# Seven block products for eight in the second layer's first multiplication, its sums by DMA

## The chip, the cores and the metric

One core of a Trainium2 chip runs the whole program. The metric is the time of one execution on the device, in microseconds; the figure for a kernel is the median of its runs. PE is TensorE, DVE is VectorE, ACT is ScalarE, POOL is GpSimd, SP the queue of SyncE.

## The reference

```python
# retention, then two gated layers; all float32 in the result
state = gamma * state + k[:, :, t] (x) v[:, :, t]          # per head, 768 steps
y[:, :, t] = scale * q[:, :, t] @ state
x  = y as (1536 tokens, 512)
x  = ((x @ w_a) * (x @ w_b)) @ w_out                      # 512 -> 1536 -> 512
h  = x @ w_in                                             # 512 -> 2048
g  = maximum(0.01 * h, h)
out = g @ w_out2                                          # 2048 -> 512
```

The weights arrive as 64-bit floats and are rounded to 32 bits on the chip.

## The kernel before

Activations lie transposed: a tile is 128 features by 512 tokens, so 1536 tokens are three token tiles (t = 0, 1, 2). Each float32 operand is split into a rounded high part and a remainder, and each product is three matmuls (`mm3`, lines 247 to 251: high x high, high x low, low x high). Every matmul of the two layers so has the line 249, 250 or 251; it moves 512 columns, or 256 where a half of token tile 1 is meant.

The stages follow each other on PE: retention until 47 us; x @ w_a and x @ w_b, twelve feature blocks, until 249 us; times w_out until 319 us; x @ w_in (here x is called y), sixteen feature blocks of 128, until 483 us; times the second w_out until the end.

Seven products for eight. The multiplications by the two w_out (class `Seven`, line 75) split tokens, the summed features and the outputs in halves, and replace eight half products by seven, p1, p7, p2, p6, p5, p4, p3, each over 6 (first layer) or 8 (second layer) steps j. One step is a product of 12 matmuls (6 of 512 columns, 6 of 256). For each, `items` (138) makes a form: three casts on ACT and three subtractions on DVE split the operands. After p1, p7 and p2 the operands themselves are summed in place (`sums`, 175, and `sum`, 117): in the first layer (`fold=True`) by DMAs that accumulate, issued by POOL (line 127), in the second by DVE (line 132). `combine` (795) adds the finished banks of p6 and p7 on DVE as soon as they are done (lines 802, 803).

The first layer's x @ w_a and x @ w_b already use seven block products for eight on the outer token tiles in feature blocks 3 to 10 (`fast`, 705): the columns of a and b are mixed and split (`sub_items`, 391), the mixed slices of x are made once (`mixed_items`, 682), and four of the products pass through one bank of PSUM, `top`, which ACT copies after the first three (723, 736, 742). Token tile 1 is done plainly. A step takes 66 matmuls of 512 columns, and one product of `Seven` is done between two steps. Tiles of the result that are not needed soon are stored to DRAM (`send`, 657) and come back later (`bring`, 665).

In the second layer x @ w_in is done plainly: `h2_step` (1054) does 12 matmuls for one token tile and one feature block, and ACT applies the rectifier (`Lrelu`, 1061) on the way out of the bank. After each feature block from the second on, one product of the second `Seven` is done, 15 in all; 41 follow.

Weights: `begin_steps` (289) has three ACT instructions (296, 299, 301: magnitude, sign, low word), `round_steps` (305) three of DVE (315 clamp, 317 shift and sign in one, 321 integer addition). Two blocks of the second layer are rounded in the first and parked in DRAM (`PARK`, line 43).

What sets the order: each engine runs its instructions in the order in which this program emits them. Work for ACT and DVE that belongs to later steps lies in the list `queue`, each item with a cost in us; `pump(us)` (333) emits items between groups of matmuls until their costs add up to its argument, and `until` (339) empties the queue as far as a needed item. `spare` is emitted when the queue is empty. On-chip tiles come from one pool of `NSLOT` buffers.

Of the kernel before, what the change touches and what calls it, by code (L numbers as in the profile page):

```python
# [14 lines left out]
U32 = mybir.dt.uint32  # L15
I64 = mybir.dt.int64
# [3 lines left out]
P = 128  # L20
# [3 lines left out]
TT = 512  # L24
# [7 lines left out]
NSLOT = 81  # L32
# [8 lines left out]
LEAD = 3  # L41
LEAD1 = 4
PARK = (0, 0, 0, 0, 0, 0, 0, 0, 0, 0, 0, 2)
# [4 lines left out]
AWAY = {(t, f) for t in range(3) for f in FAST if t == 2 or f >= FF1 // 2}  # L48
TOP = float(np.array((255 << 20) - 1, np.int32).view(np.float32))
# [25 lines left out]
class Seven:  # L75
# [17 lines left out]
    def __init__(self, nc, half, a, btile, form_new, banks, mm3, fold=False):  # L93
        self.nc, self.half, self.a, self.btile, self.fold = nc, half, a, btile, fold
# [9 lines left out]
    def away(self, i, k, j):  # L104

        return i and (2 * i, k * self.half + j) in AWAY and k == 0

# [9 lines left out]
    def sum(self, queue, op, j, d, x0, x1):  # L117
# [5 lines left out]
        if self.fold:  # L123
            for piece in range(2):
                if self.away(*d[1:], j) and not piece:
                    continue
                queue.append((0.0, lambda piece=piece: self.nc.gpsimd.dma_start(  # L127
                    self.A(*d[1:], j)[piece], self.A(*x1[1:], j)[piece], accum_op=ALU.add
                )))
            return  # L130
        for piece, cost in enumerate((0.61, 0.34)):
            queue.append((cost, lambda piece=piece: run(*(self.A(*x[1:], j)[piece] for x in (d, x0, x1)))))  # L132
# [42 lines left out]
    def sums(self, name, j):  # L175
        a11, a12, a21, a22 = (("A", i, k) for i in range(2) for k in range(2))
        b11, b12, b21, b22 = (("B", k, o) for k in range(2) for o in range(2))
        if self.fold and name in ("p1", "p7"):
            if name == "p1":
                self.sum(self.soon, "+", j, a11, a11, a21)  # L180
                self.sum(self.soon, "-", j, b11, b11, b12)
            else:
                self.sum(self.soon, "+", j, a11, a11, a22)
                self.sum(self.soon, "+", j, b12, b22, b11)
                self.sum(self.soon, "+", j, a21, a21, a22)
        elif name == "p1":
            self.sum(self.soon, "-", j, a11, a11, a21)
            self.sum(self.soon, "-", j, b11, b12, b11)
        elif name == "p7":
            self.sum(self.soon, "-", j, a11, a22, a11)  # L190
            self.sum(self.soon, "-", j, b12, b22, b11)
            self.sum(self.soon, "+", j, a21, a21, a22)
        elif name == "p2":
            self.sum(self.soon, "-", j, b21, b12, b21)
            self.sum(self.later, "-", j, a12, a12, a11)
            if j == self.half - 1:
                self.soon += self.later
# [24 lines left out]
def retention_moe_kernel(ctx: ExitStack, tc: tile.TileContext, ins, out):  # L222
# [33 lines left out]
    late_wi = [("wi", f) for f in range(FF2 - 4, FF2)]  # L256
    second = [(k, f) for f in range(FF2) for k in ("wi", "wq") if (k, f) not in late_wi]
    order, parked = [("a", 0), ("b", 0)], set()
    for f in range(1, FF1 + 1):
# [5 lines left out]
    order += second + late_wi  # L265
    source = {"a": (wab, 0), "b": (wab, 1), "wo": (wo, 0), "wi": (w2, 0), "wq": (w2, 1)}
    raws, begun, rounded, dram, signs = {}, {}, {}, {}, []
    at = {"load": 0, "begin": 0, "round": 0, "due": 0.0, "queued": 0}
# [10 lines left out]
    def word16(t, dtype, i):  # L279
# [9 lines left out]
    def begin_steps():  # L289
# [5 lines left out]
        low = tmp.tile([P, TT], I32, tag="low", name=f"low{n}")  # L295
        nc.scalar.activation(u, word(raw, F32, 1), AF.Abs, scale=2.0 ** -112)
        yield
        sign = signs[n % len(signs)]
# [3 lines left out]
        begun[key] = (u, low, sign)  # L302
        at["begin"] += 1

    def round_steps():
# [4 lines left out]
        if key not in begun:  # L310
            begin_weights()
        u, low, sign = begun.pop(key)
# [30 lines left out]
    def enqueue_round():  # L343
# [15 lines left out]
        items = [(0.05, begin), (0.46, step), (0.72, step), (0.95, end)]  # L359
# [5 lines left out]
    def enqueue_split(key, keep=False):  # L365
        def high():
            weights[key] = slots.new(F32R, f"{key[0]}{key[1]}h"), slots.new(F32R, f"{key[0]}{key[1]}l")
            nc.scalar.copy(weights[key][0], rounded[key])

        def low():  # L370
            src = rounded.pop(key)
            if key[0] == "a" and keep:
# [9 lines left out]
        behind.extend([(0.05, high), (0.05 if key[0] == "a" and keep else 0.61, low)])  # L382

    def enqueue_next(f):
        for k in "ab":
            enqueue_round()
            enqueue_split((k, f), f in FAST)
# [3 lines left out]
    def sub_items(f):  # L391

        def run(d, x, y):
            nc.vector.tensor_sub(*(kept[k, f][:, i * QT:(i + 1) * QT] for k, i in (d, x, y)))

        for d, x, y in (
            (("a", 0), ("b", 0), ("a", 0)),
            (("b", 0), ("b", 1), ("b", 0)),
            (("b", 1), ("b", 1), ("a", 0)),
            (("a", 1), ("a", 1), ("b", 1)),  # L400
# [3 lines left out]
        for k in "ba":  # L404
            def high(k=k):
                weights["t" + k, f] = slots.new(F32R, f"t{k}{f}h"), slots.new(F32R, f"t{k}{f}l")
                nc.scalar.copy(weights["t" + k, f][0], kept[k, f])

            def low(k=k):
                nc.vector.tensor_sub(weights["t" + k, f][1], kept.pop((k, f)), as32(weights["t" + k, f][0]))  # L410
# [3 lines left out]
            yield 0.61, low  # L414

# [27 lines left out]

    def ahead(rate, reserve, end):
        at["due"] = min(at["due"] + rate, 3.0)
        while at["due"] >= 1 and at["round"] < min(at["load"], end) and slots.room() >= 1 + reserve:
            round_weights()
            at["due"] -= 1
            if at["begin"] < min(at["load"], end):
                begin_weights()  # L450
# [204 lines left out]
    far, back = {}, []  # L655

    def send(t, f):

        if (t, f) in AWAY:
            far[t, f] = park.tile([P, TT], F32, tag=f"h{t}{f}", name=f"far{t}{f}")  # L660
            nc.gpsimd.dma_start(far[t, f], h[t, f])  # L661
            h[t, f] = far[t, f]
            slots.done(1)

    def bring(reserve=0):

        for key in list(far)[:1]:
            if slots.room() <= reserve:
                return
            h[key] = slots.new(F32, f"h{key[0]}{key[1]}")  # L670
            nc.sync.dma_start(h[key], far.pop(key))
            if key[0] == 2 and key[1] < FF1 // 2:
                back.append(key)

    def add_back():
        for _, f in back:
            nc.gpsimd.dma_start(h[2, f], h[2, f + FF1 // 2], accum_op=ALU.add)
        back.clear()

    S = {}  # L680

    def mixed_items():
# [9 lines left out]
        for j in range(2):  # L692
            for n, key in ((1, (2, 2 + j)), (3, (2, j)), (2, (0, j)), (4, (0, 2 + j))):
                def high(n=n, key=key, j=j):
                    S[n, j] = slots.new(F32R, f"s{n}{j}h"), slots.new(F32R, f"s{n}{j}l")
# [9 lines left out]
    def fast(f):  # L705

        def product(ps, key, half, xs, first, more):
            w = weights[key, f]
# [4 lines left out]
        copy, mul, add = nc.scalar.copy, nc.vector.tensor_mul, nc.vector.tensor_add  # L713
        a, b = range(2), range(2, KC)
        for t in range(NTILE):
            h[t, f] = slots.new(F32, f"h{t}{f}")
        want("a", f)
        pa = bank(f"pa{f}")
        ab_mm(pa, 1, f, 0, a)
        yield  # L720
        top, left = bank(f"top{f}"), bank(f"left{f}")
        product(top, "a", 0, [x[0, 0], x[0, 1]], True, False)
        copy(h[0, f], top)
        product(left, "a", 1, [x[0, 2], x[0, 3]], True, False)
        pump(2.0)
        add(h[0, f], h[0, f], left)
        ab_mm(pa, 1, f, 0, b)
        signed(h[1, f], pa, 1)
# [4 lines left out]
        until(lambda: ("ta", f) in weights and ("a", f) not in kept)  # L733
        product(top, "tb", 1, [S[2, 0], S[2, 1]], False, True)
        u = slots.new(F32, f"u{f}")
        copy(u, top)
        mid, pb = bank(f"mid{f}"), bank(f"pb{f}")
        product(mid, "ta", 0, [S[1, 0], S[1, 1]], True, False)
        ab_mm(pb, 1, f, 1, a)
        pump(3.3)  # L740
        product(top, "tb", 0, [S[3, 0], S[3, 1]], False, True)
        copy(h[2, f], top)
        slots.done(4)
        slots.tick()
        ab_mm(pb, 1, f, 1, b)
        pump(0.6)
        add(h[2, f], h[2, f], mid)
        pump(0.7)
        mul(h[1, f], h[1, f], pb)
        send(1, f)  # L750
# [3 lines left out]
        product(top, "ta", 1, [x[2, 2], x[2, 3]], False, True)  # L754
        pump(1.3)
        nc.vector.scalar_tensor_tensor(h[2, f], h[2, f], -1.0, top, op0=ALU.mult, op1=ALU.mult)  # L756
        send(2, f)
        product(mid, "b", 1, [S[4, 0], S[4, 1]], False, True)
        pump(1.0)
        add(u, u, mid)  # L760
        mul(h[0, f], h[0, f], u)
        send(0, f)
        slots.done(5)
        slots.tick()

# [447 lines left out]
```

## Time and profile before

| | us |
|---|---|
| median of 3 runs | 575.17 |
| lowest, highest | 574.05, 575.22 |
| profiled execution | 574.53 |
| its span | 572.8 |
| PE busy in the span | 567.5 |
| DVE busy | 447.8 |
| ACT busy | 371.9 |
| POOL busy | 82.7 |

The span runs from the first to the last instruction that the profile holds; the execution's time has some 1.7 us around it. Busy time is summed by engine; PE's end of a matmul is modelled, so the start times of successive matmuls say more than their durations. POOL's busy time is nearly all issuing of DMAs here.

### The profile page before, as it was taken

How to read it: one execution, taken by the hardware profiler on the slowest of the kernel's cores; microseconds unless marked ns; L12 is line 12 of the kernel's file. 1: busy time of each engine (PE TensorE's matmuls, PEld its weight loads, DVE VectorE, ACT ScalarE, POOL GpSimd, SP SyncE). 2: the span in 40 equal slices, each digit the busy share in tenths (PEclk: the TensorE clock that was granted, in tenths of full speed). 3: DMA queues.
4: the chain of work that ended last, by engine and by line, in shares of the span. 5: the costliest groups of instructions: out<-in, count | busy, mean ns of one | idle time of the engine just before them, and what ended most of it. 6: DMA issues, size and time to landing. Idle time of an engine off the chain costs nothing.

```text
span 572.8 us, 9199 instructions
## 1 busy us (share of the span) xinstructions
PE 567.5 (99%) x3287; PEld 479.8 (84%) x3287; DVE 447.8 (78%) x901; ACT 371.9 (65%) x776; POOL 82.7 (14%) x104
## 2 busy tenths in 40 slices
PE   9999999999999999999999999999999999999997
PEld 5998888888888888888888888888888888888886
DVE  4986687897988876799699686776886567789992
ACT  4777466776776764787568587777673547698610
POOL 2431300103233211077700000000000000000000
PEclk9999999999999999999999999999999999999999
DMA  8994924557676554699960053434330000010111
GB/s 323 369 392 170 259 58 129 135 144 163 174 212 196 157 157 170 243 307 237 223 149 1 1 185 110 124 100 140 116 111 0 1 0 2 2 55 1 57 55 56
DMA packets 34189, 78.53 MB, mean 137 GB/s; under 512 B 3936, under 2 KB 8288, under 8 KB 34144
## 3 DMA queue, kind: packets, MB, share of 16 engines
q1 hardware_dynamic: 23040, 58.73, 30.3%
q0 software_dynamic: 10816, 18.88, 16.2%
q8 instruction: 26, 0.43, 0.3%
q10 hardware_dynamic: 288, 0.34, 0.2%
q14 instruction: 19, 0.16, 0.1%
HBM read 57.22 MB, written 8.39 MB: 115 GB/s over the span
## 4 chain that ended last, share of the span: by engine, by line
PE 99%; DVE 0%; issue 0%
PE blk L250 12%; PE blk L249 12%; PE blk L251 12%; PE h L250 8%; PE h L249 8%; PE h L251 8%; PE pa L249 3%; PE pa L250 3%; PE pb L250 3%; PE pa L251 3%; PE pb L251 3%; PE pb L249 3%; PE top L249 3%; PE top L250 3%; PE top L251 3%; PE sc L514 2%
## 5 line engine op out<-in xcount | busy, mean ns | idle before, releaser
L250 PE MATMUL blk<-form,form 128*128 128x512 f32 (+1 forms) x224 | 75.8, 338 | 0.0
L249 PE MATMUL blk<-form,form 128*128 128x512 f32 (+1 forms) x224 | 75.6, 337 | 0.0
L251 PE MATMUL blk<-form,form 128*128 128x512 f32 (+1 forms) x224 | 75.3, 336 | 0.0
L157 DVE TENSOR_TENSOR form<-g,form 128x512 fp32r<-128x512 f32 x112 | 57.3, 553 | 2.4 <-ACT form L151 0.7
L151 ACT CAST form<-g 128x512 fp32r<-128x512 f32 x112 | 52.6, 513 | 8.5 <-DVE g L132 6.4
L1061 ACT ACTIVATE g<-h 128x512 f32<-128x512 f32 x48 | 28.7, 598 | 44.2 <-PE h L251 44.2
L250 PE MATMUL blk<-forma,forma 128*128 128x512 f32 (+1 forms) x168 | 57.1, 340 | 0.1
L249 PE MATMUL blk<-forma,forma 128*128 128x512 f32 (+1 forms) x168 | 56.7, 338 | 0.0
L251 PE MATMUL blk<-forma,forma 128*128 128x512 f32 (+1 forms) x168 | 56.5, 336 | 0.0
L157 DVE TENSOR_TENSOR forma<-h,forma 128x512 fp32r<-128x512 f32 x84 | 42.9, 551 | 5.5 <-ACT forma L151 5.2
L249 PEld LDWEIGHTS blk<-form,form 128*128 128x128 f32 x224 | 42.5, 190 | 5.5
L250 PEld LDWEIGHTS blk<-form,form 128*128 128x128 f32 x224 | 42.5, 190 | 5.0
L251 PEld LDWEIGHTS blk<-form,form 128*128 128x128 f32 x224 | 42.3, 189 | 4.7
L157 DVE TENSOR_TENSOR form<-wq,form 128x256 fp32r<-128x256 f32 x56 | 23.6, 421 | 25.1 <-ACT form L151 24.5
L151 ACT CAST forma<-h 128x512 fp32r<-128x512 f32 x84 | 39.1, 512 | 5.4 <-DMA h<-h 5.2
L250 PEld LDWEIGHTS blk<-forma,forma 128*128 128x128 f32 x168 | 31.9, 190 | 4.2 <-DVE forma L157 0.7
L249 PEld LDWEIGHTS blk<-forma,forma 128*128 128x128 f32 x168 | 31.9, 190 | 4.0
L127 POOL DMA_DIRECT2D h<-h x34 | 34.0, 1102 | 8.1 <-DVE forma L157 4.1
L251 PEld LDWEIGHTS blk<-forma,forma 128*128 128x128 f32 x168 | 31.8, 189 | 3.4
L132 DVE TENSOR_TENSOR g<-g,g 128x512 f32<-128x512 f32 (+1 forms) x56 | 30.7, 571 | 0.5 <-ACT g L1061 0.5
L151 ACT CAST form<-wq 128x256 fp32r<-128x256 f32 x56 | 22.6, 404 | 5.0 <-PE blk L251 2.1
L661 POOL DMA_DIRECT2D far<-h x18 | 10.3, 574 | 98.5 <-DVE h L756 34.5
(3079 smaller groups left out, 1556.7 us busy)
## 6 DMA issues: line engine op xcount, KB each, us to landing
raw_wi<-in_w SPq DMA_DIRECT2D x16, 512.0 KB, 3.3
raw_wq<-in_w SPq DMA_DIRECT2D x16, 512.0 KB, 3.4
raw_a<-in_wab SPq DMA_DIRECT2D x12, 512.0 KB, 6.0
raw_b<-in_wab SPq DMA_DIRECT2D x12, 512.0 KB, 4.0
raw_wo<-in_wo SPq DMA_DIRECT2D x12, 512.0 KB, 5.1
far<-h POOLq DMA_DIRECT2D x18, 256.0 KB, 4.5
h<-far SPq DMA_DIRECT2D x18, 256.0 KB, 8.9
h<-far POOLq DMA_DIRECT2D x13, 256.0 KB, 8.9
```

The costliest lines, as they stand in the source:

```text
L127: queue.append((0.0, lambda piece=piece: self.nc.gpsimd.dma_start(self.A(*d[1:], j)[piece], self.A(*x1[1:], j)[piece], accum_op=ALU.add)))
L132: queue.append((cost, lambda piece=piece: run(*(self.A(*x[1:], j)[piece] for x in (d, x0, x1)))))
L151: nc.scalar.copy(h, src)
L157: nc.vector.tensor_sub(*todo.pop(0))
L249: nc.tensor.matmul(ps, w[0], x[0], start=first, stop=False, skip_group_check=more)
L250: nc.tensor.matmul(ps, w[0], x[1], start=False, stop=False, skip_group_check=more)
L251: nc.tensor.matmul(ps, w[1], x[0], start=False, stop=last, skip_group_check=more)
L514: nc.tensor.matmul(sc[h][:, c], d["k"][r, c], d["qs"][r, c], start=True, stop=True)
L661: nc.gpsimd.dma_start(far[t, f], h[t, f])
L1061: nc.scalar.activation(g[t, f], ps, AF.Lrelu, alpha=0.01)
```

## The change

Feature blocks 4 to 13 of x @ w_in are taken in five pairs (`PAIRS`), and each pair goes through the scheme that `fast` has for w_a and w_b; that scheme becomes `seven_for_eight`, with the work on each finished bank passed in. The other blocks, 0 to 3, 14 and 15, stay plain. The rectifier is `Prelu` with its slope as an operand; where a block is a sum of two banks, ACT copies the first, DVE adds the second, and ACT applies the rectifier in place. Half of the tiles of g get the opposite sign, so that all sums of g are additions, and these are done by accumulating DMAs from POOL as in the first layer, save one that stays on DVE (p2's, `here`). Tiles of g are stored to DRAM and brought back (`Away`). Eight products of the second `Seven` are done among the steps (numbers 0 to 7), 48 after them. The sums of p6's finished banks go into the queue in both layers. In rounding, sign and low word share one 32-bit tile, so that DVE shifts alone and adds once. In the first layer one more weight block is rounded and parked in each of the steps 5 to 10. The pool has 83 buffers for 81.

```diff
-NSLOT = 81
+NSLOT = 83
+PAIRS = range(2, 7)
+NWQ = (1, 3, 1, 1, 1, 1, 1, 4)
+SOON = 9
+FORM2 = ((), (), (0,), (1,), (2,), (3,), (4,), (5, 6))
+MAKE2 = ((), (), (0,), (1,), (2,), (3,), (4,), ())
+STEP2 = {(7, 1): 5, (7, 3): 6, (7, 5): 7}
+NMADE2 = 8
-PARK = (0, 0, 0, 0, 0, 0, 0, 0, 0, 0, 0, 2)
+PARK = (0, 0, 0, 0, 0, 1, 1, 1, 1, 1, 1, 2)
+AWAY2 = {(t, f) for t in range(3) for f in range(2 * PAIRS[-1] + 2) if t == 2 or f >= FF2 // 2}
...
         for piece, cost in enumerate((0.61, 0.34)):
-            queue.append((cost, lambda piece=piece: run(*(self.A(*x[1:], j)[piece] for x in (d, x0, x1)))))
+            if self.away(*d[1:], j) and not piece:
+                continue
+            if here:
+                queue.append((cost, lambda piece=piece: run(*(self.A(*x[1:], j)[piece] for x in (d, x0, x1)))))
+                continue
+            queue.append((0.0, lambda piece=piece: self.nc.gpsimd.dma_start(
+                self.A(*d[1:], j)[piece], self.A(*x1[1:], j)[piece], accum_op=ALU.add
+            )))
...
-        nc.scalar.mul(word16(sign, F16, 1), word(raw, F32, 1), 2.0 ** -100)
+        nc.scalar.mul(half(sl, F16, 1), word(raw, F32, 1), 2.0 ** -100)
         yield
-        nc.scalar.mul(low, word(raw, U32, 0), 2.0 ** -29)
+        nc.scalar.mul(half(sl, U16, 0), word(raw, U32, 0), 2.0 ** -29)
...
-        nc.vector.scalar_tensor_tensor(
-            ui, ui, 3, sign, op0=ALU.logical_shift_left, op1=ALU.bitwise_or
-        )
+        nc.vector.tensor_scalar(ui, ui, 3, None, op0=ALU.logical_shift_left)
         yield
-        nc.vector.tensor_tensor(ui, ui, low, op=ALU.add)
+        nc.vector.tensor_tensor(ui, ui, sl, op=ALU.add)
...
-        items = [(0.05, begin), (0.46, step), (0.72, step), (0.95, end)]
+        items = [(0.05, begin), (0.4, step), (0.4, step), (0.8, end)]
...
-            nc.scalar.copy(weights[key][0], rounded[key])
+            (nc.vector.tensor_copy if key[0] == "wi" else nc.scalar.copy)(weights[key][0], rounded[key])
...
+    def seven_for_eight(ka, kb, X, S, xf, ends):
+
+        s1, c11, ma, uu, u3, c22, mb, c21, c12 = ends
...
         product(top, ka, 0, [X[0, 0], X[0, 1]], True, False)
         s1(top)
         product(left, ka, 1, [X[0, 2], X[0, 3]], True, False)
         pump(2.0)
         c11(left)
         middle(pa, ka, b)
         ma(pa)
         pump(0.7)
...
         product(top, tb, 1, [S[2, 0], S[2, 1]], False, True)
         uu(top)
...
         if name == "p6":
             for m, ps in enumerate(z.acc[name]):
-                (sub if z.fold else add)(u["p1"][m], u["p1"][m], ps)
-                add(u["p7"][m], u["p7"][m], u["p1"][m])
+                p1, p7 = u["p1"][m], u["p7"][m]
+                queue.append((0.61, lambda p1=p1, ps=ps: sub(p1, p1, ps)))
+                queue.append((0.61, lambda p1=p1, p7=p7: add(p7, p7, p1)))
...
-        if n in (2 * H1 + 1, 4 * H1):
+        if n == 2 * H1 + 1:
             enqueue_round()
...
+    def leaky(d, src, t):
+
+        plus = {0: TT, 1: QT, 2: 0}[t]
+        if plus:
+            nc.scalar.activation(d[:, 0:plus], src[:, 0:plus], AF.Prelu, alpha=0.01)
+        if plus < TT:
+            nc.scalar.activation(d[:, plus:], src[:, plus:], AF.Prelu, scale=-0.01, alpha=100.0)
...
-        nc.scalar.activation(g[t, f], ps, AF.Lrelu, alpha=0.01)
...
+    def summed():
+        while sums2:
+            t, f = sums2.pop(0)
+            leaky(g[t, f], g[t, f], t)
+            gs.send(t, f)
+
+    def fast2(f):
+
+        def s1(top):
+            nc.scalar.copy(g_new(0, f), top)
+            summed()
+
+        def total(t, f, ps):
+            nc.vector.tensor_add(g[t, f], g[t, f], ps)
+            sums2.append((t, f))
+
+        def straight(t, f, ps):
+            leaky(g_new(t, f), ps, t)
+            gs.send(t, f)
+
+        def u3(top):
+            nc.scalar.copy(g_new(2, f + 1), top)
+            summed()
...
+        return seven_for_eight(("wi", f), ("wi", f + 1), y, SY, yf, (
...
+        if q in PAIRS:
+            now = fast2(f)
+            next(now)
+            if before:
+                next(before, None)
+                make2(MAKE2[q - 1])
+            next(now)
+            before = now
...
+            if q == HALF - 1:
+                fetch(1, 6)
+                for _ in range(2):
+                    gs.bring(6, False)
...
+    for n in range(NMADE2, len(z.plan) - 2):
+        for _ in range(2):
+            gs.bring(8, n >= 2 * HALF)
+        if n >= 2 * HALF:
+            gs.add_back(4 if n < 4 * HALF - 6 else 0)
...
+        pump(1.0)
```

## Rows read from the trace of the kernel before

**Rows 1.** Page, part 4: chain that ended last, by engine.

```profile
PE 99%; DVE 0%; issue 0%
```

**Rows 2.** Timeline of PE, x w_in: start us, us, engine, line, instruction.

```profile
339.11 0.40 PE L249 MATMUL h<-y000h,wi2h 128*128 128x512 f32 x1
...
347.30 0.39 PE L249 MATMUL blk<-form,form 128*128 128x512 f32 x1
...
349.37 0.40 PE L249 MATMUL h<-y000h,wi3h 128*128 128x512 f32 x1
```

**Rows 3.** Windows: length, busy (count) PE PEld DVE ACT POOL, clock, DMA share, GB/s.

```profile
112.55:231.98 119.43, 119.43 (x545) 99.39 (x544) 98.73 (x184) 79.25 (x151) 26.22 (x36) 1.00 0.63 173
...
249.14:318.67 69.53, 69.46 (x399) 60.68 (x398) 63.51 (x143) 47.05 (x114) 28.16 (x33) 1.00 0.74 157
318.67:483.15 164.48, 164.48 (x768) 137.83 (x767) 116.13 (x227) 108.68 (x210) 0.00 (x0) 1.00 0.24 77
483.15:569.45 86.30, 85.84 (x491) 75.19 (x490) 70.96 (x160) 49.05 (x119) 0.00 (x0) 1.00 0.09 33
```

**Rows 4.** Windows of two steps of seven products, first layer.

```profile
146.67:163.74 17.07, 17.07 (x80) 14.19 (x79) 15.78 (x30) 13.59 (x27) 4.87 (x7) 1.00 0.68 180
163.74:180.80 17.06, 17.06 (x80) 14.24 (x79) 13.96 (x28) 11.68 (x23) 4.39 (x6) 1.00 0.66 181
```

**Rows 5.** Timeline of PE at the first of two gaps.

```profile
290.75 0.39 PE L249 MATMUL blk<-forma,forma 128*128 128x512 f32 x1
291.17 0.50 PE L250 MATMUL blk<-forma,forma 128*128 128x512 f32 x1
```

**Rows 6.** Groups by line: busy us, mean ns | idle before, releaser.

```profile
L157 DVE TENSOR_TENSOR form<-g,form 128x512 fp32r<-128x512 f32 x112 | 57.3, 553 | 2.4 <-ACT form L151 0.7
...
L1061 ACT ACTIVATE g<-h 128x512 f32<-128x512 f32 x48 | 28.7, 598 | 44.2 <-PE h L251 44.2
L157 DVE TENSOR_TENSOR form<-wq,form 128x256 fp32r<-128x256 f32 x56 | 23.6, 421 | 25.1 <-ACT form L151 24.5
...
L299 ACT ACTIVATE sign<-raw_wi 128x512 f16<-128x512 f32 x16 | 12.5, 782 | 0.0
...
L317 DVE SCALAR_TENSOR_TENSOR wi<-wi,sign 128x512 int32<-128x512 int32 x16 | 11.1, 692 | 1.3 <-ACT sign L299 0.8
...
L321 DVE CUSTOM_DVE_ANT_0 wi<-wi,low 128x1024 uint16<-128x1024 uint16 x16 | 11.1, 691 | 0.8
...
L296 ACT ACTIVATE wi<-raw_wi 128x512 f32<-128x512 f32 x16 | 10.6, 660 | 0.0
...
L632 ACT ACTIVATE h<-pa 128x256 f32<-128x256 f32 (+1 forms) x16 | 7.0, 440 | 1.3 <-PE pa L251 1.3
...
L315 DVE TENSOR_SCALAR wi<-wi 128x512 f32<-128x512 f32 x16 | 6.7, 421 | 4.0 <-ACT wi L296 3.9
...
L726 DVE TENSOR_TENSOR h<-h,left 128x512 f32<-128x512 f32 x8 | 5.4, 679 | 0.0
...
L1061 ACT ACT_TABLE_LOAD x1 | 1.3, 1283 | 0.0
```

**Rows 7.** Timeline: copy of `top`, PE's next write there, two steps.

```profile
149.69 0.58 ACT L723 COPY h<-top 128x512 f32<-128x512 f32 x1
...
150.46 0.40 PE L249 MATMUL top<-s20h,tb6h 128*128 128x512 f32 x1
...
165.01 0.59 ACT L723 COPY h<-top 128x512 f32<-128x512 f32 x1 [0.17 <-PE top L251]
...
167.53 0.39 PE L249 MATMUL top<-s20h,tb7h 128*128 128x512 f32 x1
```

**Rows 8.** Source line 127, DMA sums: ns min/median/max, who waited, landing.

```profile
L127 POOL DMA_DIRECT2D h<-h x34: 853/1006/2634, 129.6 to 286.3; - x34
...
  ACT forma L151: 5.2, 4
...
DMA to landing us min/median/max: 4.5/8.3/11.6
```

More of the change, by code (lines that the diff above doesn't have):

```diff
@@ L711, in product, with middle @@
                 mm3(ps, (w[0][:, c], w[1][:, c]), xs[j], first and j == 0, j == 1, more)
-        copy, mul, add = nc.scalar.copy, nc.vector.tensor_mul, nc.vector.tensor_add
-        a, b = range(2), range(2, KC)
[L715 to L719, printed above, removed]
+        def middle(ps, key, kcs):
+            w = weights[key]
+            for kc in kcs:
+                c = slice(kc * P, (kc + 1) * P)
+                mm3(ps, (w[0][:, c], w[1][:, c]), X[1, kc], kc == 0, kc == KC - 1)
+        a, b = range(2), range(2, KC)
+        want(*ka)
+        pa = bank("pa")
+        middle(pa, ka, a)
         yield
[L721 to L724, printed above, removed]
+        top, left = bank("top"), bank("left")
+        product(top, ka, 0, [X[0, 0], X[0, 1]], True, False)
+        s1(top)
+        product(left, ka, 1, [X[0, 2], X[0, 3]], True, False)
         pump(2.0)
-        add(h[0, f], h[0, f], left)
-        ab_mm(pa, 1, f, 0, b)
-        signed(h[1, f], pa, 1)
+        c11(left)
+        middle(pa, ka, b)
+        ma(pa)
         pump(0.7)
@@ L732, in fast @@
             spare.pop(0)[1]()
[L733 to L739, printed above, removed]
+        until(lambda: ta in weights and ka not in kept)
+        product(top, tb, 1, [S[2, 0], S[2, 1]], False, True)
+        uu(top)
+        mid, pb = bank("mid"), bank("pb")
+        product(mid, ta, 0, [S[1, 0], S[1, 1]], True, False)
+        middle(pb, kb, a)
         pump(3.3)
-        product(top, "tb", 0, [S[3, 0], S[3, 1]], False, True)
-        copy(h[2, f], top)
+        product(top, tb, 0, [S[3, 0], S[3, 1]], False, True)
+        u3(top)
         slots.done(4)
         slots.tick()
-        ab_mm(pb, 1, f, 1, b)
+        middle(pb, kb, b)
         pump(0.6)
-        add(h[2, f], h[2, f], mid)
+        c22(mid)
         pump(0.7)
-        mul(h[1, f], h[1, f], pb)
-        send(1, f)
+        mb(pb)
         slots.tick()
@@ L993, in leave_part @@
             y_split(i, o, m, sums[m])
-            if op:
+            if m < 2:
+                if not op:
+                    yf[0, m] = slots.new(F32, f"yf{m}")
+                    nc.scalar.copy(yf[0, m], sums[m])
+                else:
+                    yf[2 * i, 2 * o + m] = sums[m]
+            elif op:
                 slots.done(1)
@@ L1132, in retention_moe_kernel, with make2 @@
-    for n in range(FF2 + 1, FF2 + LEAD - 1):
-        z.prep(n)
-    for n in range(FF2 - 1, len(z.plan) - 2):
+    def make2(ns):
+        for n in ns:
+            until(lambda: n in z.forms)
+            z.product(n)
+            pump(1.8)
+            queue.extend(z.soon)
+            z.soon.clear()
+    spare.extend(mixed_items(yf, SY, "r"))
+    before = None
+    for q in range(HALF):
+        f = 2 * q
+        for key in (("wi", f + 2), ("wi", f + 3)) if q + 1 < HALF else ():
+            if key in dram:
+                obtain(key)
+            if key not in rounded:
+                enqueue_round()
+            enqueue_split(key, q + 1 in PAIRS)
+        forms = list(FORM2[q])
+        if q == HALF - 1:
+            queue.extend(z.items(forms.pop(0)))
+        for n in range(max(NWQ[q], len(forms))):
+            if n < NWQ[q]:
+                enqueue_round()
+            if n < len(forms):
+                queue.append((0.0, lambda m=forms[n]: queue.__setitem__(slice(0, 0), z.items(m))))
+        queue.extend(behind)
+        behind.clear()
+        if q + 1 in PAIRS:
+            queue.extend(sub_items(("wi", f + 2), ("wi", f + 3)))
+        if q in PAIRS:
[6 more added lines that the diff above has]
+            before = now
+            if q == PAIRS[-1]:
+                make2(MAKE2[q])
+                next(now, None)
+                summed()
+                slots.done(16)
+                slots.tick()
+            continue
+        if q > PAIRS[-1]:
+            gs.arrange()
+        steps = [(t, f + i) for i in range(2) for t in range(NTILE)]
+        if not q:
+            steps = [(2, 0), (2, 1), (0, 0), (1, 0), (0, 1), (1, 1)]
+        for n, (t, ff) in enumerate(steps):
+            h2_step(t, ff, all(k[1] != ff for k in steps[n + 1:]))
+            slots.tick()
+            pump(2.5)
+            if q == HALF - 1:
+                fetch(1, 6)
+                for _ in range(2):
+                    gs.bring(6, False)
+            if (q, n) in STEP2:
+                make2([STEP2[q, n]])
+                if n == 1:
+                    queue.extend(z.items(NMADE2 - 1))
+                if n == 3:
+                    for m in range(LEAD):
+                        queue.extend(z.items(NMADE2 + m))
+                    queue.append((0.7, lambda: (z.early(LEAD), z.early(LEAD + 1))))
+        if q == HALF - 1:
+            keep(z, u2, "p1")
+        slots.tick()
```

300 lines of the change are left out of this document (148 added, 152 removed).

## The prediction

> **What bounds the kernel now.** The page's chain that ended last is PE for 99% [rows 1]. The page itself warns that a busy PE need not be a PE at its peak, so the second view was the order of time on PE [rows 2]. There the reader sees matmuls of 512 columns of x w_in: 36 of them from 339.11 to 347.30, so one each 0.2275 us, and then one product of the second large multiplication to 349.37, 2.07 us. Nothing lies between. The stages [rows 3] say the same: TensorE has the granted clock 1.00 (2.4 GHz) and is busy throughout, while in the stage of x w_in DVE is busy for 116.1 and ACT for 108.7 of 164.5 us. So a change gains here only if matmuls go, or one of the few gaps; and it loses where another engine delivers late.
>
> **What goes.** For each pair of feature blocks the outer token tiles (0 and 2) are now done with seven block products for eight. Of 2 blocks x 3 tiles x 4 slices x 3 matmuls = 72, the 24 of the middle tile stay and the other 48 become 7 x 2 x 3 = 42. Five pairs lose 5 x 6 = 30 matmuls of 512 columns. The same scheme already runs in the first layer, so its price on PE can be read: a step of it lasts 17.06 us [rows 4] and holds 66 such matmuls and one product, (17.06 - 2.07)/66 = 0.227 us each; the scheme adds nothing between them. 30 x 0.227 = 6.8 us.
>
> **A gap that goes.** In the first layer's multiplication PE waits twice for DVE, at 291.17 and in the same way at 293.58. The first of these starts 0.42 us after the one before [rows 5], not 0.2275, and the second 0.43: together 0.4 us. Ahead of the late operand DVE sums the finished banks of p6, six instructions at the 0.68 of an addition from PSUM [rows 6], 4.1 us in a row; the change puts these in the queue, one behind each product, and also rounds one weight block less in this stage. Then 0.4 us goes; 0 if the operand is late for ACT's sake.
>
> **What is added on PE.** Seven products that stood between the steps of x w_in move behind them. Between steps one costs 2.07 [rows 2], 41 in a row 86.30/41 = 2.10 [rows 3]: 7 x 0.03 = 0.2 us.
>
> **The other engines, second layer.** One step of a pair with its product is 66 x 0.227 + 2.07 = 17.06 us of PE. DVE, by [rows 6], a half width at 0.421, a full one in SBUF at 0.553, from PSUM at 0.679: three roundings of 0.421 + shift + 0.691; four half-width mixes, 1.7; four splits, each a copy and a subtraction; three sums from PSUM, 2.0; one form, 0.553 + 2 x 0.421; a half-width sum of w_out. The shift alone and the copy are not in the trace. The shift lies between 0.421 (one operand, as the clamp) and 0.692 (as now, with two), the copy between 0.421 and 0.553; I take 0.421 for both, since one operand in SBUF is the nearest. That makes 4.6 + 1.7 + 3.9 + 2.0 + 1.4 + 0.4 = 14.0 us, at the upper ends 15.4. ACT, a full width at 0.598 and a half at 0.440: three roundings of 0.660 + 0.782 + the third, between 0.660 and 0.782 (a 16-bit write as the second; taken), 6.7; a form 0.598 + 2 x 0.440 = 1.5; three copies of a bank, 1.8; the rectifier on four tiles and on four halves, 4.2. The slope operand's own cost is not in the trace; 0.44, a half, and 0.782, the dearest full width, bound it, and I take 0.598, the present rectifier. Together 14.2 of 17.06. Both fit. On the other side 48 sums of g leave DVE, 24 full at some 0.68 and 24 half at 0.42, 26 us in all. In their place POOL, which does nothing in these two stages [rows 3], issues 40 accumulating DMAs and 8 that add the parked tiles back.
>
> Two waits are new. The rectifier of a summed tile stands on ACT behind the next copy of a bank and waits for DVE's addition, with the next rounding queued behind it; the addition was emitted a group of products (1.4 us) earlier and takes 0.68, so I cost the wait at nothing, at most 0.7 where DVE is an instruction late, which falls into ACT's slack of 2.9 a step. And 26 tiles of g leave by POOL and come back on SP's queue, 12 of them before p2 reads them some 8 products (17 us) later; with the 8.3 us that DMAs take here [rows 8] they are in time, and behind them on SP stand only loads of w_out that were parked. The DMA engines are used for 0.24 and 0.09 of these stages.
>
> **First layer.** Six more blocks are rounded and parked, one in each step from block 5 to 10. Seven steps now have DVE busy for 98.7 and ACT for 79.3 of 119.4 us [rows 3], 14.1 and 11.3 a step. One rounding more, with the cheaper shift in all, gives DVE + 1.53 - 3 x 0.27 = 14.8 (15.9 if the shift stays at 0.692) and ACT + 2.2 + 3 x 0.12 = 13.9, also below 17.06. The parking is one issue on a POOL of which 26 of 119 us are used.
>
> **Where the cover is thin.** The average is not the test. The bank `top` takes four products in turn, and after the first ACT must have copied it before PE writes on: PE has two groups of six matmuls, 2.7 us, to do meanwhile. In the step where ACT was busy for 11.7 us the copy ended at 165.60 and PE came at 167.53: 1.9 us to spare. In the step where ACT was busy for 13.6 us it ended at 150.27 and PE came at 150.46: 0.19 us to spare [rows 4, 7]. By the sums above all eleven steps of both layers will have ACT at about 14. So I expect the copy close to its limit in all of them; with a scatter of a few tenths about a tenth of a microsecond each is lost, 1 us (an estimate from these rows). Its bounds are 0, and 2.0 a step, a whole rounding of 2.2 ahead of the copy less the 0.19: 22 us. I take the end that the rows are near.
>
> **POOL and the sums by DMA.** Sums of g now wait on POOL's queue, behind sends that wait for ACT's rectifier. The issue took 0.85 to 2.63 us, the middle value 1.0, and 8.3 us to land [rows 8]. p7 needs 24; the last that p6 reads is the 23rd, 23 x 1.0 + 8.3 = 31 us after the first, and that operand is wanted 23 products, 48 us, after it. In the first layer, with 18 sums and four products less between, ACT waited 5.2 us for such DMAs [rows 8] and PE lost 0.4 at most. I cost it at nothing; the cover is gone if an issue takes over (48 - 8.3)/23 = 1.7 us. The Trainium skill speaks against this part: in SBUF — State Buffer, section SBUF: two separate sides, it says that a DMA issued from GpSimd starves while DVE copies fp32 in SBUF in its two-port mode, and gives 620 ns alone and some 3100 ns beside such a copy. By its figure the 23 would take 71 us and be some 31 us late (an estimate from that page). The trace bears out a spread, not that mean: with DVE busy for 63.5 of 69.5 us [rows 3] the middle value stayed at 1.0.
>
> **Sum.** From the profiled execution, 574.53 us (span 572.8 and 1.7 around it): - 6.8 - 0.4 + 0.2 + 1.0 = - 6.0, 568.5 us. The median of the runs shown is 575.17, the lowest 574.05; the profiled one lies between, so I leave the number.
>
> **Rivals.** (1) Part of the gain is given back: the queue's order makes weights or copies late in some steps, 3 us more: 571.5. For it speaks the margin of 0.19 us [rows 7], against it seven steps at 17.06 with DVE at 83%. (2) Slower: ACT's copy of `top` is late in most steps because a rounding stands ahead of it. If half of the eleven steps have the margin 0.19 and half 1.9, a rounding of 2.2 costs 5.5 x 2.0 + 5.5 x 0.3 = 12.7 us: 567.5 + 12.7 = 580.2. It decides against the change from 7 us, 0.6 a step. For it rows 7, against it that ACT is idle for 3 us of 17. (3) Sums late: at the longest issue 23 x 2.63 + 8.3 = 69 us against 48, p6 waits 21 us, 589. (4) The new rectifier needs another table than copies and roundings. Now one load of 1.283 us stands before the first rectifier and none after [rows 6], with copies in between. If the two shared no table, some five groups a pair and 18 tiles outside would switch twice each, 86 x 1.283 = 110 us on an ACT with about 30 to spare: 80 us more, about 650. By the Trainium skill, ScalarE: Activation LUTs, section Table sets: the hidden batching unit, cheap functions stand in every set and only a change of set costs a load; the single load agrees for the present rectifier, and no row shows the new one. (5) More tiles are live at once, and a new one waits for the store of an old one, up to 8.3 us. One such wait would eat the gain: 574.5.
>
> **How the numbers follow.** Forecast 0.64, (1) 0.20, (2) 0.07, (3) 0.03, (4) 0.02, (5) 0.04. The forecast's own range is 567.0 (nothing late, and 0.5 less in all) to 570.0. For 8 in 10 the range must take in (1) to a microsecond above its value: 567.0 to 572.5. What this measurement can tell from no change is 0.2%, 1.2 us: faster means below 574.0. Forecast, (1) and half of (5) are faster, 0.86; the rest of (5) and 0.03 of (2), where it takes about 7, are the same, 0.05; the rest of (2), (3) and (4) are slower, 0.09.
>
> **What would show it.** PE should have 30 matmuls less; a pair of x w_in with a product should last 17.1 us; the two waits near 291 should be gone; POOL should be busy in the second layer; one table load. If the pairs last 18 us or more with PE waiting for `top`, rival 2 is true; if p6's forms wait for DMA, rival 3. The prediction is wrong if PE's gaps in the eleven steps add up to more than 4 us, or if no gap appears and the time is still above 570.

## The result, and the profile after

The changed kernel takes 566.81 us, median of four (566.14 to 567.27), beside 574.82 for the kernel before in the same runs: ratio 0.9861, 95% interval 0.9844 to 0.9878. That is 8.0 us less, where 6.0 to 6.7 were forecast (568.5 from 574.53 or 575.17), and 0.2 us below the range. The interval, put as a time, goes from 565.9 to 567.8, so this run does not tell the 0.2 from the range's end at 567.0. The page after, its span and part 1:

```profile
span 565.1 us, 9509 instructions
...
PE 559.8 (99%) x3257; PEld 473.7 (84%) x3257; DVE 449.1 (79%) x938; ACT 382.1 (68%) x802; POOL 144.9 (26%) x186
```

PE has the 30 matmuls less (3257 for 3287). The stages (length, busy time of PE, PEld, DVE, ACT, POOL, clock, DMA share, GB/s), as in [rows 3]:

```profile
112.80:232.20 119.40, 119.40 (x545) 99.36 (x544) 102.43 (x200) 91.48 (x169) 29.63 (x42) 1.00 0.74 213
...
249.40:318.30 68.90, 68.90 (x398) 60.62 (x398) 61.48 (x138) 46.63 (x113) 26.85 (x31) 1.00 0.82 179
318.30:461.30 143.00, 143.00 (x654) 119.26 (x653) 106.13 (x216) 95.63 (x190) 33.55 (x49) 1.00 0.60 177
461.30:562.30 101.00, 100.54 (x575) 88.06 (x574) 83.86 (x193) 59.33 (x147) 25.75 (x30) 1.00 0.56 126
```

The reader sees POOL come to work in both stages of the second layer, ACT go from 79.3 to 91.5 us in the seven steps of the first, and PE without idle time everywhere. Three steps of pairs of x w_in, windows as in [rows 4]:

```profile
371.80:388.86 17.06, 17.06 (x79) 14.23 (x79) 16.34 (x35) 13.64 (x27) 3.51 (x5) 1.00 0.65 173
388.86:405.92 17.06, 17.06 (x79) 14.23 (x79) 13.93 (x30) 11.79 (x24) 5.13 (x8) 1.00 0.73 209
...
422.98:440.04 17.06, 17.06 (x79) 14.21 (x79) 6.38 (x13) 7.84 (x17) 7.53 (x11) 1.00 0.92 303
```

They last 17.06 us, as the first layer's, though DVE is busy for 16.34 of them in the first of these. The two gaps of [rows 5] are gone. Where the cover was thought thin, at the copies of `top`, the instructions stand as follows, as in [rows 7]: one step of the first layer (block 6) and the second pair of the new stage.

```profile
148.21 0.59 ACT L801 COPY h<-top 128x512 f32<-128x512 f32 x1
...
150.73 0.39 PE L249 MATMUL top<-s20h,tb6h 128*128 128x512 f32 x1
...
374.67 0.57 ACT L1125 COPY g<-top 128x512 f32<-128x512 f32 x1
...
375.51 0.39 PE L249 MATMUL top<-r20h,twi7h 128*128 128x512 f32 x1
```

Block 6, where 0.19 us were to spare, now has 150.73 - 148.80 = 1.93; the new pair has 0.27. Single instructions against [rows 6] (mean ns):

```profile
L304 ACT ACTIVATE sl<-raw_wi 128x512 uint16<-128x512 uint32 x16 | 12.4, 772 | 0.0
...
L320 DVE TENSOR_SCALAR wi<-wi 128x512 int32<-128x512 int32 x16 | 6.8, 425 | 0.4
...
L1095 ACT ACTIVATE g<-top 128x512 f32<-128x512 f32 x5 | 2.9, 587 | 4.8 <-PE top L251 4.8
...
L866 ACT ACT_TABLE_LOAD x1 | 1.3, 1283 | 1.2 <-DVE warm L863 1.2
```

The shift alone takes 425 ns, the third rounding instruction 772, the rectifier 587 from a full bank: all near the values that were taken. The one table load stands at the start of the kernel (L866), where the kernel before has one as well; the one before the first rectifier is gone. The DMA sums of g (line 138), as in [rows 8]:

```profile
L138 POOL DMA_DIRECT2D g<-g x26: 860/1274/2871, 379.3 to 482.1; - x26
L138 POOL DMA_DIRECT2D g<-farg x14: 868/932/2787, 378.7 to 470.8; - x14
...
DMA to landing us min/median/max: 3.0/8.1/13.7
```

Where the 7.7 us between the two profiled spans lie, read from the starts of PE's instructions: from the first matmul of the first layer to the first of x w_in 273.92 before and 273.32 after (-0.60); from there to the last matmul of the kernel 247.99 and 241.19 (-6.80); from the end of the last addition to the end of the span (the tail) 3.31 and 2.76 (-0.55); the first matmul of the first layer starts at 46.80 and 47.05 (+0.25).

### The profile page after: what moved, and what is told of

Read it like the earlier page. It is cut to its first block, busy times and chain, and to the rows that moved or that the text cites. A ratio compares the mean times of both kernels' runs of the same rounds, so it can differ in the third digit from the quotient of the medians.

```text
span 565.1 us, 9509 instructions
## 1 busy us (share of the span) xinstructions
PE 559.8 (99%) x3257; PEld 473.7 (84%) x3257; DVE 449.1 (79%) x938; ACT 382.1 (68%) x802; POOL 144.9 (26%) x186
## 4 chain that ended last, share of the span: by engine, by line
PE 97%; DMA 2%; POOL 0%; SPq 0%; DVE 0%; issue 0%
PE blk L250 12%; PE blk L249 12%; PE blk L251 12%; PE top L249 4%; PE top L250 4%; PE top L251 4%; PE pa L249 4%; PE pa L250 4%; PE pb L250 4%; PE pa L251 4%; PE pb L249 4%; PE pb L251 4%; PE h L249 3%; PE h L251 3%; PE h L250 3%; PE mid L249 2%
## 5 line engine op out<-in xcount | busy, mean ns | idle before, releaser
L663 POOL DMA_DIRECT2D farg<-g x26 | 14.4, 557 | 114.0 <-ACT g L1095 97.6
L138 POOL DMA_DIRECT2D g<-g x26 | 29.5, 1651 | 3.2 <-DVE form L165 1.3
L663 POOL DMA_DIRECT2D farh<-h x18 | 10.3, 575 | 59.9 <-DVE h L791 36.1
```

What stands on the lines that cost most here:

```text
L663: nc.gpsimd.dma_start(self.far[t, f], self.tiles[t, f])
```

## The experiments

An experiment without a ratio is one profiled execution; it is read by stretches of its trace and not by its time.

**The changed kernel and the kernel before once more** (no edit).

> The changed kernel itself, once more. Theory: 30 matmuls (6.8 us) and two waits of PE (0.6) are all that the change gives, 7.4 us; the other 0.3 to 0.6 of the 8.0 between the medians is scatter at the beginning and the end of an execution. Then the ratio in five rounds is near 1 - 7.4/574.8 = 0.987, TensorE again enters x w_in 312 to 314 us before its last matmul with no gap of its own, and the start and the tail differ from the first profile by up to 0.5 us. Rival: some 0.6 us more are gained in a step that I have not seen; then the start and the tail repeat to 0.1 us and the ratio is 0.986 or less.

> The kernel before, once more, for the scatter of one profile against another: the first matmul of the first layer at 46.9 us and 3.35 us from the last addition to the end of the span in the first profile. Theory (scatter): both move by 0.2 to 0.5 us. Rival (the change moved them): both repeat to 0.1.

The changed kernel took 567.1 (ratio 0.987, 0.9852 to 0.9889), just inside the predicted range. Its profile has 273.28, 241.20 and 2.77 us for the three stretches; that of the kernel before has 274.16, 247.99 and 3.33. The first matmul of the first layer moved between 46.72 and 48.14: that is scatter. The first stretch of the kernel before moved too, by 0.24: its two waits are longer here, and the change gains 0.88 us in this stretch for 0.60 in the first pair of profiles. The tail did not move: 2.76 and 2.77 after, 3.31 and 3.33 before, so the scatter theory is wrong for it and the change has 0.55 us more there.

**Where the first layer's gap comes from.** One edit of the change each in the kernel before:

```diff
-                (sub if z.fold else add)(u["p1"][m], u["p1"][m], ps)
-                add(u["p7"][m], u["p7"][m], u["p1"][m])
+                p1, p7, op = u["p1"][m], u["p7"][m], sub if z.fold else add
+                queue.append((0.61, lambda p1=p1, ps=ps, op=op: op(p1, p1, ps)))
+                queue.append((0.61, lambda p1=p1, p7=p7: add(p7, p7, p1)))
...
+            until(lambda: name == "p2")
...
+        pump(1.0)
```

> The kernel before with one part of the change: the sums of p6's finished banks go through the queue, one or two behind each product, in both layers. Theory: PE's two waits at 291 and 294 us came from DVE doing six of these sums in a row ahead of the next form; they go, 0.6 us. Rival: the operand was late because ACT rounded a weight block at that place (and waited for a DMA before it); then the waits stay.

```diff
-        if n in (2 * H1 + 1, 4 * H1):
+        if n == 2 * H1 + 1:
```

> The kernel before with another part of the change: the second rounding of a weight block during the first layer's w_out (behind product 24) is left out there and done in the next stage. Theory (DVE's sums made the operand late): the two waits near 291 and 294 stay, perhaps shorter by the 1.8 us of DVE that the rounding takes there. Rival (the rounding on ACT did): they go, 0.6 us.

With the queue alone, PE at the place of the two gaps:

```profile
291.16 0.40 PE L249 MATMUL blk<-forma,forma 128*128 128x512 f32 x1
291.39 0.40 PE L250 MATMUL blk<-forma,forma 128*128 128x512 f32 x1
...
293.26 0.40 PE L249 MATMUL blk<-forma,forma 128*128 128x512 f32 x1
293.49 0.40 PE L250 MATMUL blk<-forma,forma 128*128 128x512 f32 x1
```

The next matmul comes after 0.23 us. From the first layer's start to x w_in it is 273.46 us (0.22 are lost at 306 instead); without the rounding 273.40, with one gap of 0.1 us left. Neither theory is the whole of it, and DVE in the trace of the kernel before shows why:

```profile
286.13 0.68 DVE L802 TENSOR_TENSOR up<-up,blk 128x512 f32<-128x512 f32 x1
...
290.43 1.02 DVE L157 TENSOR_TENSOR forma<-h,forma 128x512 fp32r<-128x512 f32 x2
291.37 0.42 DVE L315 TENSOR_SCALAR wq<-wq 128x512 f32<-128x512 f32 x1
291.89 0.69 DVE L317 SCALAR_TENSOR_TENSOR wq<-wq,sign 128x512 int32<-128x512 int32 x1
292.50 0.42 DVE L157 TENSOR_TENSOR forma<-wo,forma 128x256 fp32r<-128x256 f32 x1
292.84 1.02 DVE L157 TENSOR_TENSOR forma<-h,forma 128x512 fp32r<-128x512 f32 x2
```

Ahead of the first wait stand the six sums, from 286.13 to 290.18, and ahead of them a form for which ACT's cast had waited for a DMA. That DMA landed 236.3 us after the first matmul here, 236.5 in the second profile of the kernel before, 236.1 without the rounding, and the wait was 0.30, 0.57 and 0.14 us. Ahead of the second wait stand clamp and shift of the rounding, 1.1 us of DVE between two forms: without the rounding it is gone. With the sums in the queue both are gone (the DMA landed at 236.1 there too).

**Fewer and more pairs.**

```diff
-PAIRS = range(2, 7)
-STEP2 = {(7, 1): 5, (7, 3): 6, (7, 5): 7}
+PAIRS = range(2, 6)
+STEP2 = {(6, 2): 4, (7, 1): 5, (7, 3): 6, (7, 5): 7}
```

> The changed kernel with four pairs for five: blocks 12 and 13 of x w_in are done plainly again. Theory (the stage gives exactly what its matmuls cost): from the first matmul of x w_in to the last of the kernel 241.20 + 6 x 0.227 = 242.56 us, no gap of PE. Rival (a part of the gain comes from the order of the work and not from the count of matmuls): the difference is 0.5 us or more away from 1.36. The end of the span behind the last addition, 2.8 us for 3.35 before, stays at 2.8 if it belongs to the program's shape and not to this stage.

249.21 us, of which 6.6 are lost in a single stretch: product 4, which had to find another place, came before its form (PE waited 2.5 us for ACT), and the matmuls behind it were slow (last section). The rest is 242.6, as expected from the matmuls; the order of the work decided the other 6.6. The tail was 2.65.

```diff
-PAIRS = range(2, 7)
+PAIRS = range(1, 7)
```

> The changed kernel with six pairs for five: blocks 2 and 3 too go through the scheme. Theory: 1.36 us less, 239.84 us from the first matmul of x w_in to the last, time about 565.6, if the mixed slices of y are ready; they and the mixed weights of the pair must now be made beside the first plain pair alone, 16.4 us of PE, with DVE at about 17 us of work there. So up to 2 us of waiting in the first step are possible, and the gain is between 1.4 and -0.6. Rival (the cover at the start of the stage is gone): PE waits 3 us or more before the first product on mixed slices, and the kernel is slower than with five pairs.

566.9 (0.9866, 0.985 to 0.9883), 241.38 us: the 1.36 us were won and lost again, 1.25 of them at one place, where PE waits for DVE's sum of the bank `mid`:

```profile
366.15 0.39 PE L251 MATMUL top<-y111h,twi4l 128*128 128x512 f32 x1
367.52 0.50 PE L249 MATMUL mid<-r40h,wi5h 128*128 128x512 f32 x1 [0.98 <-DVE g L1129]
```

DVE was busy for 16.1 of 17.1 us there. Two kernels moved DVE's work away from it:

```diff
-NWQ = (1, 3, 1, 1, 1, 1, 1, 4)
+NWQ = (3, 1, 1, 1, 1, 1, 1, 4)     # pairs6d
+NWQ = (1, 1, 0, 1, 2, 2, 2, 4)     # pairs6e
...
+            else:
+                pump(2.0)
```

> Six pairs, with two roundings of w_out moved from beside block pair 1 to beside pair 0, and 2.0 us of the queue emitted between the first two groups of the first pair. Theory (with six pairs DVE is full at the start of the stage, 14.4 of 14.9 us and 16.1 of 17.1, and the sum that PE waits for at 367.5 us stands behind the mixing of the next pair's weights): DVE starts the pair earlier and PE's wait of 1.3 us falls to 0.5 or less. But DVE beside pair 0 has only 2.6 us free and the two roundings need 3.1, so a part of the wait may come back there. Rival (the wait comes from the order of the queue alone): it stays at 1 us or more.

> Six pairs, with three roundings of w_out moved from beside pairs 1 and 2 to beside pairs 4 to 6, where DVE has 3 to 10 us free, and the same 2.0 us of the queue. Theory (the stage costs exactly its matmuls while DVE has room in each step): no gap of PE, 241.2 - 1.36 = 239.84 us from the first matmul of x w_in to the last, ratio to before 0.987 - 0.0024 = 0.9846, and the kernel is the fastest. Rival (the gain of the sixth pair is lost for another reason, ACT's copies or tiles): 240.5 us or more.

Moved ahead (pairs6d), the mixing of y on DVE was late: PE waited nearly 9 us at once, and the stretch took 252.42. Moved behind (pairs6e), the gap at that place is gone, and two others of 1.45 and 1.24 us come beside blocks 10 and 11: 242.59, ratio 0.988 (0.9864 to 0.9897). Without them it is 239.9, as expected. The second is again a sum of `mid` behind DVE's mixing. At the first PE waits for a copy of ACT, and ahead of that ACT had waited for a tile (ACT's waits in pairs 3 to 6: total us, times, longest):

```profile
ACT g L1125 <- DMA farg<-g: 2.0, 1, 2.0
```

ACT's copy of `top`, 5.7 us before the late one, waited for the store of an old tile of g: that is rival 5 of the prediction. That this wait alone made the later copy late was not tested. No version with six pairs is faster than five.

**The cover of the copies of `top`.**

```diff
+        for _ in range(2):                   # act4: 4
+            nc.scalar.copy(idle, as32(X[1, 0][0]))
         s1(top)
```

> The changed kernel with two idle copies of 512 columns put on ACT ahead of the first copy of the bank top in all thirteen steps, some 1.0 us. Theory (the copy has its own margin in each step, and only steps with a small one pay): the margins in the trace of the changed kernel are 0 in the step of block 4, 0.27 in the second pair, 1.0 in block 5 and 1.7 to 1.9 in the ten others, so PE loses 1.0 + 0.7 = 1.7 us. Rival of the prediction (the load of ACT sets the margin, all steps are close): ten steps or more pay, 8 us or more. Second rival (ACT makes it up from its idle time): under 0.5 us.

> The same with four idle copies, some 2.0 us. Theory (margins of single steps): block 4 pays 2.0, the second pair 1.7, block 5 1.0, block 3 0.3, the others up to 0.1 each: 5 to 6 us. Rival (load of ACT): 16 us or more, since ACT is then at 15 to 16 of 17.06 us in each step. Second rival (made up): under 1 us.

Two idle copies took 1.24 us, not 1.0. PE lost 2.8 us, in three steps: block 4, 1.46; the second pair, 1.06; block 5, 0.26. The first of these, in the trace of act2:

```profile
116.47 1.24 ACT L739 CAST idle<-x10h 128x512 bf16<-128x512 f32 x2
...
117.62 0.58 ACT L804 COPY h<-top 128x512 f32<-128x512 f32 x1
...
118.25 0.50 PE L249 MATMUL top<-s20h,tb4h 128*128 128x512 f32 x1 [1.20 <-ACT h L804]
```

PE comes 0.05 us after the copy has ended. The other ten steps paid nothing (block 3 paid 0.06). Four took 2.4 us, more than the margin of 1.93, and now every step but one paid: blocks 5 to 9, four of them with 1.93 us to spare, 0.6 each, block 4 2.8, the second pair 2.4, the others 0.2 to 1.5; in all 14 us, of which 3.2 are slow matmuls behind the two longest waits (last section). That is more than the 5 to 6 expected, because an idle copy was longer than I had put it and because of the clock, and it cannot tell the two theories apart. act2 can: among the ten steps that took 1.24 us more without a loss are blocks 6 to 8, where ACT is busy for 13.7 us in the changed kernel, and the second pair, which paid, has 13.64. The margins of single steps decide, not the load of ACT.

**Twice the clamp.**

```diff
         nc.vector.tensor_scalar(u, u, TOP, None, op0=ALU.min)
+        nc.vector.tensor_scalar(u, u, TOP, None, op0=ALU.min)
```

> The changed kernel with the clamp of each rounding done twice: 0.42 us more of DVE for each of the 80 weight blocks, more than the shift alone has saved (0.27). Theory (DVE has the room that the sums gave it): a step goes from about 14.6 to 16.3 us of 17.06 in the first layer and from 14.0 to 15.3 in the second, and PE loses under 0.5 us. Rival (the cheaper rounding is a needed part of the gain): PE loses 3 us or more, mostly in the first layer's steps with four roundings.

244.29 us for 241.20, and 0.6 in the first layer (the kernel has 68 weight blocks, not 80). 2.2 us are waits in the second pair, 1.9 of them one wait; this is the step whose DVE was at 16.34 of 17.06:

```profile
387.37 0.68 DVE L1130 TENSOR_TENSOR g<-g,mid 128x512 f32<-128x512 f32 x1
...
388.11 0.50 PE L249 MATMUL mid<-r40h,wi7h 128*128 128x512 f32 x1 [1.60 <-DVE g L1130]
```

The other 0.9 us are no wait: from about 470 us on each product takes 2.12 us for the 2.10 of the other runs, and no row says why. So the waits are 2.7 us in all, more than the theory's 0.5 and less than the rival's 3, and mostly not in the first layer where I looked for them. That the cheaper shift is a needed part is argued and not shown: the second clamp adds 0.42 us a block, and the shift alone saves 0.27; but that step has four roundings, and four times 0.27 is more than the 0.72 us that DVE had left in it.

**Idle DMAs behind each sum of g.**

```diff
+            if self.here:
+                for _ in range(1):           # pool2: 2
+                    queue.append((0.0, self.more))
```

`more` stores 128 KB of an idle tile to DRAM.

> The changed kernel with one idle DMA of 128 KB to DRAM on POOL behind each of the 40 sums of g, 0.55 us of issue each. Theory (sums by DMA have a cover that ends where an issue takes 1.7 us): the 24 sums of p7 end 24 x 0.55 = 13 us later, about 495 for 482 us, land at 503, and the last that p6 reads is wanted by its form at about 503: PE loses 0 to 2 us. Rival (the cover is already used up, since ACT waits 4.2 us for one of these DMAs in the changed kernel): 5 us or more.

> The same with two idle DMAs behind each sum, 1.1 us of issue. Theory: an issue with its followers takes over 2.3 us, beyond 1.7; the last sum lands 26 us later than in the changed kernel, at about 516 for a product that starts at 510 and a form some 6 us before it: PE loses 6 to 14 us. Rival (the order of POOL does not reach PE at all): under 1 us.

With one, p7's sums leave POOL every 1.58 us: 241.25 us, nothing lost. With two they leave every 2.17: 251.67, 10.5 us more, of which 6.4 are waits and some 4 slow matmuls behind two of them (last section). The cover of 1.7 us an issue lies between the two. The trace of pool2 shows the chain of the first long wait, from POOL's issue, which landed at 511.94, to PE:

```profile
508.05 1.25 POOL L138 DMA_DIRECT2D g<-g  x1
...
511.96 0.62 ACT L162 CAST form<-g 128x512 fp32r<-128x512 f32 x1 [3.20 <-DMA g<-g]
...
512.63 0.50 PE L252 MATMUL blk<-form,form 128*128 128x512 f32 x1 [2.56 <-ACT form L162]
```

The second long wait, 2.75 us at 519.72, hangs on a DMA that adds a parked tile back, issued by POOL behind all these.

**One buffer less.**

```diff
-NSLOT = 83
+NSLOT = 82
```

> The changed kernel with 82 buffers in the pool for 83. Theory (no new tile waits for the store of an old one, there is room of a buffer or more): no gap of PE, 241.2 us from the first matmul of x w_in to the last. Rival 5 of the prediction (tiles are short): some wait of up to 8 us appears where the pool is full.

PE lost 0.85 us in the first layer's w_out, waiting for a form of DVE, and why that form was late stays open. It lost 0.6 in the stage, and there it is the rival: ACT's copy waits for a tile whose old content is still on its way to DRAM:

```profile
410.09 0.59 ACT L1125 COPY g<-top 128x512 f32<-128x512 f32 x1 [2.71 <-DMA farg<-g]
...
410.73 0.50 PE L249 MATMUL top<-r20h,twi11h 128*128 128x512 f32 x1 [0.30 <-ACT g L1125]
```

With 83 buffers that wait is not there: the pool is just large enough. The tail was 3.47 us, with the last store 0.7 us slower to land.

## Why the prediction was wrong, point by point

- The 30 matmuls: 6.8 us expected, 6.80 and 6.79 measured in the two pairs of profiles. Right.
- The gap: 0.4 expected, 0.60 and 0.88 measured. I had counted only the late matmul; the one behind it starts 0.1 us late as well, both times (291.17 to 291.51 in the trace of before). Of the two reasons given, the six sums belong to the first wait and the rounding to the second.
- What is added on PE: 0.2 expected, nothing measured. Between steps the slower starts behind a product (0.235 for 0.227 us) fall on the matmuls of the step, and my difference of 2.10 and 2.07 counted them as if they were saved there.
- **Where the cover is thin: 1.0 us of loss expected, 0.05 measured (block 4). This is the term of the sum that failed most.** I read the 0.19 us of block 6 as what a busy ACT does, and gave all eleven steps that load. I had looked at two steps. Block 5 in the same trace has ACT busy for only 10.83 us, and the copy ends at 132.49 with PE at 133.40, 0.9 to spare. After the change blocks 5 and 6 have more load than block 6 had then, and margins of 1.03 and 1.93. ACT's load is the fourth busy time of each line; the first line is the kernel before:

```profile
129.60:146.67 17.07, 17.07 (x80) 14.24 (x79) 13.47 (x27) 10.83 (x22) 4.21 (x6) 1.00 0.73 170
...
129.88:146.94 17.06, 17.06 (x80) 14.23 (x79) 15.46 (x32) 14.47 (x29) 5.71 (x8) 1.00 0.93 245
146.94:164.00 17.06, 17.06 (x80) 14.23 (x79) 14.79 (x30) 13.74 (x26) 4.43 (x7) 1.00 0.70 191
```

In block 6 the same rounding, form and split stand on ACT ahead of the copy before and after; they now begin 1.9 us earlier, counted from the first layer's start. What sets a margin is where the queue puts this work, and act2 settles it: a step pays by its own margin, whatever the load.
- **The end of the span, 0.55 us, was in no term; it was put at nothing without a reason.** It repeats: 3.31 to 3.33 in four profiles of the kernel before and its variants, 2.65 to 2.78 in eleven with the change and 83 buffers. The last store lands 1.74 us after the last addition in both. Behind that, SP waits for eight semaphores of its DMAs one after another, in the same order in every trace, some 0.06 us each. The last store reports to the second of them before and to the sixth after, and SP is done 0.45 and 0.20 us after the landing (0.08 with four pairs, where it is the eighth): this is 0.25 us, and luck, since nothing in the change aims at it. The other 0.30 is a pause of POOL in the closing sequence, 0.34 us before and 0.04 after; why POOL pauses stays open.
- The range's low end had no loss at the cover and 0.5 us to spare. The gap's 0.2, the products' 0.2 and the tail's 0.55 are 0.45 more than that: 6.80 + 0.60 + 0.55 = 7.95, where the range ended at 7.53 below 574.53. In the first pair of profiles a later start took 0.25 back; the medians differ by 8.0 and 8.1.
- POOL: nothing lost, as costed; the point from which it loses was tested from both sides. The sums of p7 left POOL every 1.01 us, as costed, though the middle issue of g<-g lasted 1.27 us (mean 1.65) for the 1.0 I had read: issues overlap in the trace. ACT waited once, 4.2 us, for a DMA that adds a parked tile back, and PE did not.
- Rival 4 was the other way round: the new rectifier needs no load of its own.
- DVE and ACT in the pairs: 13.8 to 16.3 and 11.8 to 13.6 in the second to the fourth, 14.0 and 14.2 expected. The mean hid the second pair, the thinnest place of the kernel for DVE.

## What to carry to other kernels

Where PE never waited, the removed matmuls came back to the hundredth of a microsecond, and the same scheme elsewhere in the trace gave the price. What a busy helper engine costs is not read from its load but from the margin of each hand-over, step by step, and two steps are not enough to read it from; and a margin in the trace of before belongs to its order of work, which the change replaces. Where a step has no room, another unit of the same gain is lost again: at DVE, then at a tile.

## What the runs showed of the hardware

TensorE's clock fell in four experiments, each time behind a long wait of PE: 2.5 us with four pairs, 2.5 and 2.1 with four idle copies, 2.6 and 2.8 with two idle DMAs, 8.7 in pairs6d. In the kernel with four pairs PE started one matmul between 428.9 and 432.9:

```profile
426.00:428.90 2.90, 2.90 (x14) 2.25 (x12) 2.54 (x6) 2.90 (x7) 0.00 (x0) 1.00 0.51 179
428.90:431.60 2.70, 0.21 (x1) 0.00 (x0) 2.53 (x6) 2.70 (x7) 0.00 (x0) 1.00 0.70 214
431.60:432.90 1.30, 0.50 (x1) 0.19 (x1) 1.30 (x4) 0.28 (x1) 0.54 (x1) 0.65 0.98 342
432.90:439.00 6.10, 6.00 (x17) 5.01 (x18) 0.72 (x3) 0.00 (x0) 1.79 (x2) 0.51 0.87 291
439.00:442.00 3.00, 3.00 (x15) 2.44 (x14) 0.00 (x0) 0.60 (x1) 0.00 (x0) 1.00 1.12 274
```

After two waits, of 2.5 and 0.9 us, the granted clock was 0.51 (1.2 GHz of 2.4) for 6 us, and matmuls of 512 columns started every 0.43 us for 0.227; then it was 1.00 again. The shortest wait with such a fall is the 2.1 us in the second pair of act4:

```profile
387.30:389.70 2.40, 0.30 (x2) 0.00 (x0) 2.23 (x6) 2.34 (x5) 0.00 (x0) 1.00 0.79 261
389.70:393.70 4.00, 3.99 (x11) 3.14 (x12) 3.47 (x8) 2.74 (x7) 2.37 (x3) 0.57 0.51 122
```

Behind the wait of 1.6 us in the kernel with the double clamp it stayed:

```profile
386.00:388.20 2.20, 0.60 (x4) 0.18 (x2) 2.17 (x6) 2.20 (x5) 0.00 (x0) 1.00 0.64 130
388.20:392.00 3.80, 3.80 (x20) 3.26 (x21) 3.53 (x9) 2.90 (x5) 1.13 (x2) 1.00 0.88 293
```

A wait of PE may therefore cost twice: of the 6.6 us of the four-pair kernel some 2.8 are the slow matmuls.
